# Filling batches of an attention loop: a new order inside each turn, rotating exponential banks, a wait on the third exponential, and weight preparation one turn earlier

## The chip, the cores and the metric

The kernel runs on one core of a Trainium2 chip. The metric is the device time of one execution in microseconds (us). The profile names the engines PE (matrix products), PEld (PE loading the stationary operand of a product), DVE (vector), ACT (activations), POOL (GpSimd) and SP (it issues most DMAs); "PEclk" or "granted clock" is the share of PE's full clock.

## The reference

One transformer block with adaptive layer norm, on 2048 rows of 512 numbers, all in 32-bit floats:

```python
mod = (_silu(c) @ w_mod).reshape(c.shape[0], 6, 1, -1)     # sa, ca, ga, sb, cb, gb
h = _layernorm(x) * (1 + ca) + sa
x = x + ga * attention(h)      # 32 query heads of 16, one key head, one value head, softmax, then @ wo
h = _layernorm(x) * (1 + cb) + sb
x = x + gb * (gelu(h @ w1 + b1) @ w2 + b2)                 # 512 -> 1376 -> 512
```

## The kernel before

**Units and turns.** The 2048 query rows are cut into 8 blocks of 256, and each block into 8 units of four heads: 64 units. A unit's scores are built transposed, 128 keys by 512 query columns at a time. The operands of a score product have 64 rows, so it uses one half of the PE array; `s` (0 or 1) says which half. Two products on different halves run at the same time, and two on the same half one after the other.

For each unit the loop from line 1289 takes the keys in steps: `K` counts 8 steps, two of them (`X`, `Y`) in one pass through the loop body. A pass has two **turns**. In each, PE gets products on both halves, side by side, and then `pv` (line 589), the 16 instructions `acc` that multiply the exponentials by the values; they use all rows of the array and write tile `acc`. The `pv` after the first turn is that of the step before, the one after the second turn is that of `X`.

The products of a turn are of three kinds:

- `sexp` (line 571): one product `e` (line 584), a bank of 512 scores, and at once `p` (line 587), its exponential on ACT. There are four in a turn. They use three banks, `e0`, `e1` and `e2`; the number is written out by hand where `sexp` is called (lines 1324 to 1348). A product into a bank waits for the ACT instruction that read the bank last.
- `Max.step` (line 483): one product `m` (line 490) for a *later* unit, whose softmax needs the maximum of each row first, and the reduction `mx` (line 495) on DVE. There are four in nearly every turn. Tag `m` has three banks, in rotation; each `m` waits for the reduction of the third `m` before it. When a unit's maxima are complete, `put_max` has POOL gather them and SP send them to rows of `qst`, from where the exponentials get them.
- `half` (line 179): **fillings**. All other matrix work (query projections `qps`, output projection `wops`, transposes `tp`, the two feed-forward layers `w1ps` and `w2ps`) is cut into batches of about six products of 512 columns. A batch's products have 128 rows; the first turn of a pass does rows 0 to 63 of each of them, on half 0, beside the score products of half 1, and the second turn does rows 64 to 127, on half 1, beside the score products of half 0. Both halves add to one PSUM bank. A turn without a batch is **plain** (`plain`, line 1308): it has only four `e` and about four `m`.

**What sets the order.** Every engine runs its instructions in the order in which they are written. `issue` (line 1260) merges two or more groups: it takes the next instruction of the group whose summed lengths are smallest, and the first group of those that tie. `mixture` (line 1270) alternates two lists. In a filled turn one group is the score half (`m`, `e`, `m`, `e`, `m`, `e`, `m`) and the other the six halves and then one `e`. `halves` (line 1302) gives the halves their lengths, with `AHEAD` = 0.75 for a full batch. The score group comes first, unless the batch begins a new bank. PE's order in a filled turn is then

```
m e h h m h e h m h h e e m        # h: a filling
```

where the thirteenth instruction, an `e`, runs on the fillings' half and the others, but for `h`, on the score half. After the last half batch of a bank, `resume` issues the instruction that empties the bank, mostly on DVE, and the reductions collected in `reduces` come behind it.

**Waits for weight pieces.** `clock` counts four ticks a pass. The first layer's weights are split into two parts in advance and kept in DRAM (`dw1`); `fetch_w1` (line 745) brings a piece back, and `heed` notes its DMA with a due tick (6 ticks later). `wait_early` (line 567) lets an `e` of the second turn of a pass wait for the first noted DMA that is due. `fetch_rest` (line 749) fetches the first three pieces, once for each block.

**Weight preparation.** `prep_w1`, `prep_wo` and `prep_w2` (lines 1029 to 1080) are advanced once a pass (every `PREP` = 4 ticks). In `prepare` (line 1018) piece `i` is loaded at one call, split on POOL (`work`) two calls later, and, for `w1`, sent to DRAM two calls after that. The staging tile has three buffers.

Of the kernel before, what the change touches and what calls it, by code (L numbers as in the profile page):

```python
# [47 lines left out]
def adaln_mqa_mlp(  # L48
# [127 lines left out]
        for ps, a, b_, first_, last_ in batch:  # L176
            nc.tensor.matmul(ps, a, b_, start=first_, stop=last_)  # L177

    def half(one, s):

        ps, a, b_, first_, last_ = one
        rows = slice(64 * s, 64 * s + 64)
        nc.tensor.matmul(ps, a[rows], b_[rows], start=first_ and s == 0, stop=last_ and s == 1)  # L183

    def ln_stats(xt, pool, n, between=None):
        st = pool.tile([P, n, 6], F32, name="st", tag="st", bufs=2)
# [369 lines left out]
    accs = {}  # L556
    heeded = []

    def wait_for(ins, other, reason):
        tc.add_manual_dep(ins.ins, other.ins.name, mybir.DependencyInfo(mybir.DependencyClass.Sync, mybir.DependencyReason.DATA),  # L560
                          reason=reason)

    def heed(dma, n):

        heeded.append((clock[0] + n, dma))

    def wait_early(ins):
        if heeded and heeded[0][0] <= clock[0]:
            wait_for(ins, heeded.pop(0)[1], "a weight piece")

    def sexp(u, K, j, s, bank):

        w = blocks[units[u][0]][1]
# [10 lines left out]
        ins = nc.tensor.matmul(e, ks[rows, kt * P:(kt + 1) * P], rhs, start=True, stop=True)  # L584
        if clock[0] % 4 == 2 and s == 0 and K % 2:
            wait_early(ins)
        nc.scalar.activation(ptiles[u, K][:, j, s, :], e, AF.Exp, scale=0.25)  # L587

    def pv(u, K):
        w = blocks[units[u][0]][1]  # L590
        if K == 0:
            accs[u] = psum.tile([P, w], F32, name=f"acc{u}", tag="v")
        pt = ptiles.pop((u, K))
        for kt in ([K] if w == 512 else [2 * K, 2 * K + 1]):
            for cidx in range(4):
                s, j = divmod(cidx, 2)
                rhs = pt[:, j, s, :] if w == 512 else pt[:, kt - 2 * K, s, j * w:(j + 1) * w]
                nc.tensor.matmul(accs[u][32 * cidx:32 * cidx + 32, :], va[:, kt, :], rhs,  # L598
                                 start=kt == 0, stop=kt == NKT - 1)

    def finish_unit(u):
        b, Q = units[u]
# [686 lines left out]
    for u in range(NU):  # L1289
        for K in range(0, steps[u], 2):  # L1290
            goal = lead[u] + (lead[u + 1] - lead[u]) * (K + 2) / steps[u]
            goal = min(goal, first[u + QBUFS] if u + QBUFS < NU else first[NU])
            n = max(0, 2 * round((goal - mp.done) / 2))

            def maxes(s, n, first_=1.0, held=None):
                return [(1.0 if i else first_, lambda i=i: mp.step(s, held if i == 2 else None)) if mp.has(s) else (0.0, lambda: None)
                        for i in range(n)]

            def exps(s, which):
                return [(1.0, lambda K=K, j=j, bank=bank: sexp(u, K, j, s, bank)) for K, j, bank in which]  # L1300
# [7 lines left out]
            def plain(s, K, t, n, banks):  # L1308

                a, b_, c_, d = banks  # L1310
                one = mixture(exps(s, [(K, 0, a), (K, 1, c_)]), maxes(s, n))
                other = maxes(t, n)
                if not holder and mp.has(t) and n > 1:
                    other[-1] = 1.0, lambda: mp.step(t, tag="x", bufs=1)
                issue(one, exps(t, [(K, 0, b_)]) + other + exps(t, [(K, 1, d)]))

            X, Y = K, K + 1

            due()
            batch = take() if behind else None
            if batch:
                groups = [mixture(maxes(1, n // 2, 0.0), exps(1, [(X, 0, 0), (X, 1, 1), (Y, 0, 2)])),
                          halves(batch, 0) + exps(0, [(X, 0, 0)])]
                issue(*(reversed(groups) if batch[0][3] else groups))
            else:
                plain(1, X, 0, (n + 2) // 4, (1, 2, 0, 1))
            clock[0] += 1
            due()  # L1330
            if behind:
                end_step(*behind)
            clock[0] += 1
            due()
            if batch:

                reduces = [] if batch[-1][4] else None

                def go_on_():
                    resume()  # L1340
                    for fn in reduces or ():
                        fn()

                issue(mixture(maxes(0, n // 2, 0.0, reduces), exps(0, [(X, 1, 0), (Y, 0, 1), (Y, 1, 2)])),
                      halves(batch, 1) + [(0.0, go_on_)] + exps(1, [(Y, 1, 0)]))
                advance()
            else:
                plain(1, Y, 0, n // 4, (2, 0, 1, 2))
            clock[0] += 1
            due()  # L1350
            end_step(u, X)
            behind = (u, Y)
            clock[0] += 1
            if state["mods"] and state["q"] == 0 and w2H is None:
                w2H = att.tile([P, NF, D], F32R, name="w2H", tag="bigH")
                w2L = att.tile([P, NF, D], F32R, name="w2L", tag="bigL")
                preps["w2"] = prep_w2()
            if clock[0] >= prepared[0] + PREP and weights and weights[0] in preps:
                prepared[0] = clock[0]
                if next(preps[weights[0]], 0) == 0:  # L1360
                    weights.pop(0)
# [51 lines left out]
```

## Time and profile before

| | us |
|---|---|
| three runs | 1591.32, 1591.73 (median), 1595.98 |
| the profiled execution | 1592.94 |
| its span in the trace | 1590.6 |
| the attention loop in it, from the first to the last of its turns | 82.7 to 1538.3 |

What the profiled execution took beyond its span, 2.3 us, lies around the trace. The trace's clock starts with the span. A row of a timeline has start, duration, engine, line, operation and the tile written and read, and in brackets how long the engine sat idle before it and what ended that. "PEld" rows are weight loads; a product's wait is on its load. The ends of PE's rows are modelled by the profiler.

### The profile page before, as it was taken

To read this page: it belongs to the slowest core of one execution; us is meant where nothing else is said; L and a number is where in the kernel's file an instruction comes from. 1 tells how busy PE (TensorE), PEld (TensorE's weight loads), DVE (VectorE), ACT (ScalarE), POOL (GpSimd) and SP (SyncE) were. 2 spreads that over 40 slices of the span, in tenths; PEclk is the share of its full clock that TensorE was granted. 3 is DMA by queue.
4 is the path that set the end of the run, shared out by engine and by line. 5 is a ranking of instruction groups with operands and counts; after the bars stand their busy time and mean duration, and the time that the engine had idled before them with its cause. 6 is when DMAs were issued, how large, how long until landed. Compare 5 with 4: busy or idle time off the path is not lost.

```text
span 1590.6 us, 41519 instructions
## 1 busy us (share of the span) xinstructions
PE 1563.0 (98%) x16369; PEld 1008.8 (63%) x16369; DVE 1410.8 (89%) x2473; ACT 1201.1 (76%) x2393; POOL 667.5 (42%) x1176
## 2 busy tenths in 40 slices
PE   6999999999999999999999999999999999999998
PEld 3466665557665676657666676656666576656667
DVE  7899999899999998999989999999999999999615
ACT  5577778778777887778877887778877787778853
POOL 4445434747422571246421462244612473225711
PEclk8999999999999999999999999999999999999999
DMA  7236312313020220303112120303112120212231
GB/s 250 82 113 214 105 68 70 128 39 101 17 98 31 68 69 25 103 18 107 32 49 79 54 85 22 106 14 98 43 37 89 45 96 19 95 39 63 81 134 73
DMA packets 83126, 121.62 MB, mean 76 GB/s; under 512 B 19614, under 2 KB 56222, under 8 KB 82676
## 3 DMA queue, kind: packets, MB, share of 16 engines
q1 hardware_dynamic: 82916, 118.97, 23.0%
q8 instruction: 129, 2.11, 0.6%
q14 instruction: 65, 0.53, 0.1%
q10 hardware_dynamic: 16, 0.00, 0.0%
HBM read 91.13 MB, written 27.27 MB: 74 GB/s over the span
## 4 chain that ended last, share of the span: by engine, by line
PE 88%; DVE 4%; POOL 4%; ACT 2%; DMA 1%; issue 1%; SPq 0%; POOLq 0%; DVEq 0%; ACTq 0%
PE acc L598 29%; PE m L490 21%; PE e L584 17%; PE w1ps L183 8%; PE w2ps L183 4%; DVE mx L495 3%; PE wops L183 2%; POOL xh L805 2%; PE qps L183 2%; PE w2ps L177 1%; PE w1ps L177 1%; ACT p L587 1%; PE tp L183 1%; PE kps L159 1%; POOL x L809 0%
## 5 line engine op out<-in xcount | busy, mean ns | idle before, releaser
L495 DVE TENSOR_REDUCE mx<-m 128x1 f32<-128x512 f32 x2048 | 1270.1, 681 | 101.4 <-PE m L490 73.8
L587 ACT ACTIVATE p<-e 128x512 f32<-128x512 f32 x2048 | 1067.2, 599 | 308.0 <-PE e L584 240.2
L490 PE MATMUL m<-ks,qst 64*128 64x512 f32 x2048 | 819.6, 424 | 6.1 <-ACT ks L393 2.3
L584 PE MATMUL e<-qst,ks 64*128 64x512 f32 x2048 | 739.1, 409 | 3.4 <-ACT p L587 1.5
L598 PE MATMUL acc<-p,va 128*32 128x256 f32 x8192 | 548.8, 385 | 0.0
L490 PEld LDWEIGHTS m<-ks,qst 64*128 64x128 f32 x2048 | 362.8, 184 | 168.8 <-DVE mx L495 145.2
L584 PEld LDWEIGHTS e<-qst,ks 64*128 64x128 f32 x2048 | 366.0, 184 | 91.2 <-ACT p L587 64.2
L598 PEld LDWEIGHTS acc<-p,va 128*32 128x32 f32 x8192 | 213.9, 109 | 218.9 <-issue 115.6
L183 PE MATMUL w1ps<-h2H,w1t 64*128 64x256 f32 x1232 | 236.7, 288 | 0.8
L539 POOL TENSOR_SCALAR mt<-turned 8x32 f32<-8x32 f32 x256 | 53.4, 209 | 400.6 <-DVE turned L545 388.6
L183 PEld LDWEIGHTS w1ps<-h2H,w1t 64*128 64x128 f32 x1232 | 184.1, 185 | 32.8 <-issue 23.3
L183 PE MATMUL w1ps<-h2L,w1t 64*128 64x256 f32 x616 | 169.6, 275 | 0.0
L183 PE MATMUL w2ps<-w2H,gH 64*128 64x512 f32 x286 | 118.0, 413 | 0.0
L183 PE MATMUL w2ps<-w2L,gH 64*128 64x512 f32 x286 | 117.3, 410 | 0.0
L183 PE MATMUL w2ps<-w2H,gL 64*128 64x512 f32 x286 | 117.3, 410 | 0.0
L183 PEld LDWEIGHTS w1ps<-h2L,w1t 64*128 64x128 f32 x616 | 113.5, 184 | 0.0
L906 POOL TENSOR_SCALAR tt<-tt 128x256 f32<-128x256 f32 x77 | 31.2, 405 | 162.5 <-ACT tt L905 159.3
L907 POOL TENSOR_TENSOR tt<-tt,z 128x256 f32<-128x256 f32 x77 | 57.1, 741 | 6.4
L134 POOL TENSOR_TENSOR gL<-z,gH 128x256 fp32r<-128x256 f32 x77 | 56.9, 739 | 6.4
L917 POOL TENSOR_TENSOR z<-tt,z 128x256 f32<-128x256 f32 x77 | 56.3, 731 | 6.0
L916 POOL TENSOR_TENSOR tt<-tt,z 128x256 f32<-128x256 f32 x77 | 56.8, 737 | 0.0
L183 PEld LDWEIGHTS w2ps<-w2H,gH 64*128 64x128 f32 x286 | 52.7, 184 | 5.9 <-DVE ot L953 2.5
(188 smaller groups left out, 1468.0 us busy)
## 6 DMA issues: line engine op xcount, KB each, us to landing
w1t<-dw SPq DMA_DIRECT2D x82, 512.0 KB
qst<-dq SPq DMA_DIRECT2D x384, 32.0 KB
do<-oc SPq DMA_DIRECT2D x64, 128.0 KB
dw<-w1s SPq DMA_DIRECT2D x11, 512.0 KB
xt<-in_A_x_dram SPq DMA_DIRECT2D x4, 1024.0 KB
dq<-qH SPq DMA_DIRECT2D x16, 256.0 KB
dq<-qL SPq DMA_DIRECT2D x16, 256.0 KB
x<-in_A_x_dram SPq DMA_DIRECT2D x8, 512.0 KB
```

The lines of the kernel that those rows point to most:

```text
L134: eng_l.tensor_tensor(out=dst_l, in0=src, in1=raw(dst_h), op=ALU.subtract)
L177: nc.tensor.matmul(ps, a, b_, start=first_, stop=last_)
L183: nc.tensor.matmul(ps, a[rows], b_[rows], start=first_ and s == 0, stop=last_ and s == 1)
L490: nc.tensor.matmul(m, qsts[u][rows, j, t * P:(t + 1) * P], ks[rows, kc * 512:(kc + 1) * 512], start=True, stop=True)
L495: nc.vector.tensor_reduce(out=self.mx[u][:, i, kc:kc + 1], in_=m, axis=AX.X, op=ALU.max)
L539: nc.gpsimd.tensor_scalar(out=mt[:, g:g + 32], in0=turned[g:g + 4 * T, :], scalar1=1.0, scalar2=0.0, op0=ALU.mult, op1=ALU.add)
L584: ins = nc.tensor.matmul(e, ks[rows, kt * P:(kt + 1) * P], rhs, start=True, stop=True)
L587: nc.scalar.activation(ptiles[u, K][:, j, s, :], e, AF.Exp, scale=0.25)
L598: nc.tensor.matmul(accs[u][32 * cidx:32 * cidx + 32, :], va[:, kt, :], rhs, start=kt == 0, stop=kt == NKT - 1)
L907: nc.gpsimd.tensor_tensor(out=tt, in0=tt, in1=z, op=ALU.mult)
L916: nc.gpsimd.tensor_tensor(out=tt, in0=tt, in1=z, op=ALU.mult)
L917: nc.gpsimd.tensor_tensor(out=z, in0=tt, in1=z, op=ALU.add)
```

## The change

Four edits, all in or for the loop:

1. **Order and banks.** `sexp` takes its bank from `ebank()`, which rotates through the three banks over all exponentials, in place of numbers written by hand. In a filled turn the fillings' group now always stands first. The score half is built by `scores`: `m e m e m`, then the remaining `m`, then the third `e`. The lengths in `halves` are now the same for all batches: together 4.5 of the score half's units, so that the `e` of the fillings' half comes ahead of the last `e` of the score half: it is the third of the turn's four exponentials. When a bank ends with the batch, the reductions of the third *and* fourth maximum are held until the bank's emptying is issued (before: of the third).
2. **The witness.** That third exponential is kept as `state["witness"]`. The first half product of each following half batch waits for it, except the very first of a bank.
3. **Weight pieces.** The waits move from `e` to products of `pv`, any due one is taken, and the due tick is 24 ticks after the fetch for a block's first three pieces and 8 for the others (before 6).
4. **Preparation.** The split of a piece comes one call after its load (before two), and its sending two calls after the split, as before.

In plain turns, the `m` that is put into bank `x` is the first of its half, no longer the last.

PE's order in a filled turn is now `h m e h m h e h h m h m e e`, with the thirteenth again on the fillings' half.

```diff
-AHEAD = 0.75
...
-    def half(one, s):
+    def half(one, s, behind=None):
 
         ps, a, b_, first_, last_ = one
         rows = slice(64 * s, 64 * s + 64)
-        nc.tensor.matmul(ps, a[rows], b_[rows], start=first_ and s == 0, stop=last_ and s == 1)
+        ins = nc.tensor.matmul(ps, a[rows], b_[rows], start=first_ and s == 0, stop=last_ and s == 1)
+        if behind is not None:
+            wait_for(ins, behind, "the other half of the array adds to the same bank")
...
     def wait_early(ins):
-        if heeded and heeded[0][0] <= clock[0]:
-            wait_for(ins, heeded.pop(0)[1], "a weight piece")
-
-    def sexp(u, K, j, s, bank):
+        for one in heeded:
+            if one[0] <= clock[0]:
+                heeded.remove(one)
+                wait_for(ins, one[1], "a weight piece")
+                break
+
+    def sexp(u, K, j, s):
...
-        e = psum.tile([P, 512], F32, name=f"e{u}_{K}_{j}_{s}", tag="x" if bank == "x" else f"e{bank}", bufs=1)
+        e = psum.tile([P, 512], F32, name=f"e{u}_{K}_{j}_{s}", **ebank())
...
-        ins = nc.tensor.matmul(e, ks[rows, kt * P:(kt + 1) * P], rhs, start=True, stop=True)
-        if clock[0] % 4 == 2 and s == 0 and K % 2:
-            wait_early(ins)
-        nc.scalar.activation(ptiles[u, K][:, j, s, :], e, AF.Exp, scale=0.25)
+        nc.tensor.matmul(e, ks[rows, kt * P:(kt + 1) * P], rhs, start=True, stop=True)
+        return nc.scalar.activation(ptiles[u, K][:, j, s, :], e, AF.Exp, scale=0.25)
...
-                nc.tensor.matmul(accs[u][32 * cidx:32 * cidx + 32, :], va[:, kt, :], rhs,
-                                 start=kt == 0, stop=kt == NKT - 1)
+                ins = nc.tensor.matmul(accs[u][32 * cidx:32 * cidx + 32, :], va[:, kt, :], rhs,
+                                       start=kt == 0, stop=kt == NKT - 1)
+                if kt % 2 and cidx:
+                    wait_early(ins)
...
-        heed(nc.sync.dma_start(out=raw(w1ts[f]), in_=dw1[f]), 6)
+        heed(nc.sync.dma_start(out=raw(w1ts[f]), in_=dw1[f]), 8 if f > 2 else 24)
...
-        for i in range(n + (4 if send else 2)):
-            if send and i >= 4:
-                send(i - 4)
-            if 2 <= i < n + 2:
-                work(i - 2)
+        for i in range(n + (3 if send else 1)):
+            if send and i >= 3:
+                send(i - 3)
+            if 1 <= i < n + 1:
+                work(i - 1)
...
-                return [(1.0 if i else first_, lambda i=i: mp.step(s, held if i == 2 else None)) if mp.has(s) else (0.0, lambda: None)
+                return [(1.0 if i else first_, lambda i=i: mp.step(s, held if i > 1 else None)) if mp.has(s) else (0.0, lambda: None)
...
-                total = products(batch)
-                ahead = AHEAD if total > BATCH - 0.5 else (BATCH - (1.5 if batch[-1][4] else 0.5)) / total
-                return [(ahead * products([one]), lambda one=one: half(one, s)) for one in batch]
+                ahead = (BATCH - 1.5) / products(batch)
+                behind_ = None if s == 0 and batch[0][3] else state["witness"]
+                return [(ahead * products([one]), lambda i=i, one=one: half(one, s, None if i else behind_))
+                        for i, one in enumerate(batch)]
+
+            def scores(s, which, held=None):
+
+                m, e = maxes(s, n // 2, 0.0, held), exps(s, which)
+                return mixture(m[:3], e[:2]) + m[3:] + e[2:]
...
-                    other[-1] = 1.0, lambda: mp.step(t, tag="x", bufs=1)
+
+                    other[0] = 1.0, lambda: mp.step(t, tag="x", bufs=1)
...
-                groups = [mixture(maxes(1, n // 2, 0.0), exps(1, [(X, 0, 0), (X, 1, 1), (Y, 0, 2)])),
-                          halves(batch, 0) + exps(0, [(X, 0, 0)])]
-                issue(*(reversed(groups) if batch[0][3] else groups))
+                issue(halves(batch, 0) + exps(0, [(X, 0)], True), scores(1, [(X, 0), (X, 1), (Y, 0)]))
...
-                issue(mixture(maxes(0, n // 2, 0.0, reduces), exps(0, [(X, 1, 0), (Y, 0, 1), (Y, 1, 2)])),
-                      halves(batch, 1) + [(0.0, go_on_)] + exps(1, [(Y, 1, 0)]))
+                issue(halves(batch, 1) + [(0.0, go_on_)] + exps(1, [(Y, 1)], True), scores(0, [(X, 1), (Y, 0), (Y, 1)], reduces))
```

More of the change, by code (lines that the diff above doesn't have):

```diff
@@ L1295, in maxes, with exps, one, plain @@
             def maxes(s, n, first_=1.0, held=None):
[L1296 removed]
+                return [(1.0 if i else first_, lambda i=i: mp.step(s, held if i > 1 else None)) if mp.has(s) else (0.0, lambda: None)
                         for i in range(n)]
[L1299 to L1312 removed]
+            def exps(s, which, witness=False):
+                def one(K, j):
+                    ins = sexp(u, K, j, s)
+                    if witness:
+                        state["witness"] = ins
+                return [(1.0, lambda K=K, j=j: one(K, j)) for K, j in which]
+            def halves(batch, s):
+                ahead = (BATCH - 1.5) / products(batch)
[5 more added lines that the diff above has]
+                return mixture(m[:3], e[:2]) + m[3:] + e[2:]
+            def plain(s, K, t, n):
+                one, other = maxes(s, n), maxes(t, n)
                 if not holder and mp.has(t) and n > 1:
[L1314 to L1315 removed]
+                    other[0] = 1.0, lambda: mp.step(t, tag="x", bufs=1)
+                issue(mixture(exps(s, [(K, 0), (K, 1)]), one), exps(t, [(K, 0)]) + other + exps(t, [(K, 1)]))
             X, Y = K, K + 1
@@ L1323, in adaln_mqa_mlp @@
             if batch:
[L1324 to L1326 removed]
+                issue(halves(batch, 0) + exps(0, [(X, 0)], True), scores(1, [(X, 0), (X, 1), (Y, 0)]))
             else:
[L1328 removed]
+                plain(1, X, 0, (n + 2) // 4)
             clock[0] += 1
@@ L1340, in go_on_ @@
                     resume()
-                    for fn in reduces or ():
-                        fn()
-                issue(mixture(maxes(0, n // 2, 0.0, reduces), exps(0, [(X, 1, 0), (Y, 0, 1), (Y, 1, 2)])),
-                      halves(batch, 1) + [(0.0, go_on_)] + exps(1, [(Y, 1, 0)]))
+                    while reduces:
+                        reduces.pop(0)()
+                issue(halves(batch, 1) + [(0.0, go_on_)] + exps(1, [(Y, 1)], True), scores(0, [(X, 1), (Y, 0), (Y, 1)], reduces))
+                assert not reduces
                 advance()
             else:
-                plain(1, Y, 0, n // 4, (2, 0, 1, 2))
+                plain(1, Y, 0, n // 4)
             clock[0] += 1
```

6 lines of the change are left out of this document (3 added, 3 removed).

## The prediction

> **What bounds the kernel now.** The page comes first, for the engines and the two costliest groups.
>
> ```profile
> span 1590.6 us, 41519 instructions
> PE 1563.0 (98%) x16369; PEld 1008.8 (63%) x16369; DVE 1410.8 (89%) x2473; ACT 1201.1 (76%) x2393; POOL 667.5 (42%) x1176
> ...
> L495 DVE TENSOR_REDUCE mx<-m 128x1 f32<-128x512 f32 x2048 | 1270.1, 681 | 101.4 <-PE m L490 73.8
> L587 ACT ACTIVATE p<-e 128x512 f32<-128x512 f32 x2048 | 1067.2, 599 | 308.0 <-PE e L584 240.2
> ```
>
> PE is busy throughout, so time is saved only where PE's own sequence gets shorter. One maximum takes DVE 0.68 us and one exponential takes ACT 0.60 us. The attention loop is a row of turns, each closed by 16 `acc` instructions, so the windows view over line 598 counts turns (x/16). The stretches below are filled, plain, filled, plain, plain, filled.
>
> ```profile
> 82.70:243.70 161.00, 59.86 (x896) 23.37 (x896) 1.00 0.37 122
> 243.70:291.30 47.60, 19.36 (x292) 7.51 (x288) 1.00 0.29 89
> 291.30:317.80 26.50, 9.31 (x128) 3.52 (x128) 0.94 0.40 131
> 317.80:328.60 10.80, 4.40 (x68) 1.67 (x64) 1.00 0.09 20
> ...
> 340.00:345.60 5.60, 2.19 (x36) 0.83 (x32) 1.00 0.08 21
> 345.60:500.60 155.00, 57.71 (x864) 22.54 (x864) 1.00 0.21 68
> ```
>
> A turn with a filling takes 155.0/54 = 2.87 us (161/56 = 2.87 in the first stretch). The eight turns from 291.3 took 26.5/8 = 3.31 us; more on them below. Plain turns number 18, and then 4 + 2 in each of seven passes: 60. The same view over line 490 counts the turns that also hold four maximum products:
>
> ```profile
> 82.70:1538.30 1455.60, 798.25 (x1984) 354.02 (x1984) 1.00 0.22 70
> ```
>
> 1984/4 = 496 turns, less 60 plain ones, leaves **436 filled turns**; nearly all of the change lies in them. The timeline of one:
>
> ```profile
> 802.82 0.50 PE L490 MATMUL m<-ks,qst 64*128 64x512 f32 x1
> 802.86 0.50 PE L183 MATMUL w2ps<-w2H,gH 64*128 64x512 f32 x1
> 803.15 0.39 PE L584 MATMUL e<-qst,ks 64*128 64x512 f32 x1
> 803.35 2.48 DVE L495 TENSOR_REDUCE mx<-m 128x1 f32<-128x512 f32 x4 [0.35 <-PE w2ps L183]
> 803.38 0.39 PE L490 MATMUL m<-ks,qst 64*128 64x512 f32 x1
> 803.38 0.18 PEld L584 LDWEIGHTS e<-qst,ks 64*128 64x128 f32 x1
> 803.58 2.13 ACT L587 ACTIVATE p<-e 128x512 f32<-128x512 f32 x4 [0.77 <-PE w2ps L183]
> ...
> 804.07 0.39 PE L584 MATMUL e<-qst,ks 64*128 64x512 f32 x1
> 804.23 0.18 PEld L584 LDWEIGHTS e<-qst,ks 64*128 64x128 f32 x1
> 804.23 0.18 PEld L490 LDWEIGHTS m<-ks,qst 64*128 64x128 f32 x1
> 804.30 0.43 PE L490 MATMUL m<-ks,qst 64*128 64x512 f32 x1
> 804.36 0.39 PE L584 MATMUL e<-qst,ks 64*128 64x512 f32 x1
> 804.67 1.07 PE L598 MATMUL acc<-p,va 128*32 128x256 f32 x16
> 805.67 0.18 PEld L490 LDWEIGHTS m<-ks,qst 64*128 64x128 f32 x1 [0.41 <-DVE mx L495]
> 805.76 0.18 PEld L183 LDWEIGHTS w2ps<-w2H,gH 64*128 64x128 f32 x1
> ```
>
> Two halves of the array work side by side. The score half runs m, e, m, e, m, e, m; the other runs six filling halves and one e. On a half, products start 0.23 us apart (803.15, 803.38), except that the first is followed after 0.33: **a load that nothing covers costs about 0.10**. The seven starts of the score half therefore lie at 0, 0.33, 0.56, 0.79, 1.02, 1.25 and 1.48 us. A turn is then 1.85 us of products and 1.00 of `acc`.
>
> Two waits show. ACT ends at 803.58 + 2.13 = 805.71, and only then can the next turn's first e load, since it has the bank of the exponential just finished; the filling is queued behind it and loads at 805.76, 0.09 after m. And the last e loads at 804.23, 0.05 after the first exponential of its turn (803.58 + 0.60 = 804.18), whose bank it reuses.
>
> **The change, part by part.**
>
> *Rotating banks, fillings first.* The first e of a turn takes the bank of the second exponential of the turn before, long read, so the 0.09 goes. The last e now takes the bank of this turn's first exponential, so its load still cannot come before 1.41 us and the turn cannot end before 2.84: the fastest turns now, such as that between the last two loads in the next fence, 811.49 to 814.33. The gain is bounded by 2.87 - 2.84 = 0.03 a turn, 13 us in all.
>
> *The witness.* The first filling of each half batch, unless it begins a bank, waits for the third exponential of the turn before. Behind it on PE stands the whole turn. Its product is the seventh of its half: start 1.48, end 1.87, on ACT by 1.91 (the 0.04 between the e that ends at 803.54 and ACT at 803.58), done at 2.51, seen at 2.56. The next turn starts at 2.84 or later. Cost taken: nothing; the cover is 0.28 us, and a later ACT beyond it would be paid one for one, with no gain possible.
>
> *The new order of the score half.* The groups are now issued as m, e, m, e, m, **m, e**: the fourth maximum moves from the seventh place to the sixth. There are three m banks, so the fourth waits for the first maximum of its own turn. That one starts on DVE at 0.53 (803.35 - 802.82) and takes 0.68: 1.21. How soon a load follows, and what a late one costs, a turn with a disturbed DVE shows:
>
> ```profile
> 808.07 3.67 DVE L495 TENSOR_REDUCE mx<-m 128x1 f32<-128x512 f32 x6
> 808.59 0.49 PE L490 MATMUL m<-ks,qst 64*128 64x512 f32 x1
> ...
> 810.00 0.18 PEld L490 LDWEIGHTS m<-ks,qst 64*128 64x128 f32 x1 [0.19 <-DVE mx L495]
> 810.07 0.18 PEld L584 LDWEIGHTS e<-qst,ks 64*128 64x128 f32 x1
> 810.49 1.07 PE L598 MATMUL acc<-p,va 128*32 128x256 f32 x16
> 811.49 0.18 PEld L490 LDWEIGHTS m<-ks,qst 64*128 64x128 f32 x1 [0.41 <-DVE mx L495]
> ...
> 814.33 0.18 PEld L490 LDWEIGHTS m<-ks,qst 64*128 64x128 f32 x1 [0.41 <-DVE mx L495]
> ```
>
> The six maxima are (3.67 - 0.68)/5 = 0.60 apart; the third, this turn's first, ends at 808.07 + 1.20 + 0.68 = 809.95, and the load comes at 810.00: 0.05 later. Now the fourth m in its new place: loaded at 1.21 + 0.05 = 1.26, where covered loads stand at 1.02; running 0.10 later, at 1.36, not at 1.25. The third e is behind it on the same half: 1.36 + 0.23 = 1.59. From a last product to `acc` I take 0.34 (load 804.23, so running at 804.33, `acc` at 804.67). The turn is 1.59 + 0.34 + 1.00 = **2.93 us, 0.06 more than now**; in the old seventh place the load at 1.26 was just in time. Bounds: nothing, if the late load is absorbed (2.84), to a load wholly exposed at its 0.18 (3.01). I take 0.10, which the first load of every turn shows. Over 436 turns: +26.2 us.
>
> Where DVE also empties a 512-wide bank, the first maximum of the next turn is later. Three groups of these lie in the loop (of the x16, two each are in the tail):
>
> ```profile
> L953 DVE TENSOR_TENSOR ot<-w2ps,x 128x512 f32<-128x512 f32 x16 | 11.1, 691 | 23.6 <-PE w2ps L183 15.9 <-PE w2ps L177 7.8
> L786 DVE TENSOR_TENSOR x<-wops,x 128x512 f32<-128x512 f32 x16 | 11.1, 691 | 2.3 <-PE wops L183 1.2 <-PE wops L177 0.8 <-PE m L490 0.2
> ...
> L441 DVE COPY q<-qps 128x512 f32<-128x512 f32 x14 | 9.7, 691 | 0.2
> ```
>
> That makes 42 turns. In the example the maximum ended at 809.95 - 808.59 = 1.36, less 0.06 for the longer turn ahead: 1.30, so 0.09 beyond the 1.21 already counted: +3.8 us. (Such turns were dearer before too; that is within the mean of 2.87.)
>
> The Trainium skill, "TensorE: Matmul & The Clock Gate", Part 3, "What overlaps and what doesn't", says that a weight load overlaps running matmuls only if its row group differs. By that rule the late load is exposed in full, 0.18 us, with the sum of the second rival below. The trace is against it: at 803.38 an e loads while m of the same half runs.
>
> *Weight pieces awaited later.* The waits of line 585 on the first fetched pieces stall PE in the eight turns from 291.3:
>
> ```profile
> 301.90 0.18 PEld L584 LDWEIGHTS e<-qst,ks 64*128 64x128 f32 x1 [1.43 <-DMA w1t<-dw]
> ...
> 303.18 0.22 PEld L584 LDWEIGHTS e<-qst,ks 64*128 64x128 f32 x2 [0.75 <-DMA w1t<-dw]
> ```
>
> With 24 ticks (twelve turns, 34 us) instead of 6 the pieces have landed: 8 x (3.31 - 2.87) = -3.5 us, the slower clock there (0.94) included. Later fetches show no such wait, so 8 instead of 6 is nothing.
>
> *Preparation a turn sooner.* Loads, splits and sends keep their number. A split now follows its load by two turns (5.7 us), not four. The longest wait of this kind now:
>
> ```profile
> POOL w2f L1077 <- DMA w2f<-in_B_w_dram: 3.7, 1, 3.7
> ```
>
> Behind a waiting split stand the gathers of the maxima on POOL, and behind those, SP's sends of them; the exponentials that need them start most of a unit (eight turns) later. That cover takes a delay of 3.7 us. Taken: nothing; if it failed, about 3.7 us at a unit boundary. Plain turns keep their order but for which maximum has bank x: nothing.
>
> **Sum.** +26.2 + 3.8 - 3.5 = +26.5 us on the profiled execution's 1592.9 us: 1619.4. That execution stands 1.2 us above the median of the runs, 1591.7, so I predict **1618 us**.
>
> **Rivals.**
>
> *The late load is absorbed.* If the first maximum is seen early enough, by about 1.15 instead of 1.26, or PE has slack that I miss, all filled turns fall to 2.84: 436 x -0.03 = -13.1, -3.5 more: 1575 us. For it: the waits that go are real. Against it: 0.53 + 0.68 is the same in every turn, however the turn before ran.
>
> *The late load is exposed in full.* Turns of 3.01: 436 x 0.14 = +61.0, with +3.8 - 3.5: 1653 us. Against it: the 0.33 after the first product.
>
> *The witness binds.* It decides from the point where the third exponential is seen after the turn's end, 0.37 us later than reckoned for a turn of 2.93. Activations of the feed-forward stand at the head of ACT's turns and could do that; ACT now waits 0.77 us there, which speaks against it. At 0.1 us in every turn it would be +44 us beyond the forecast: 1661.
>
> *Gain and loss cancel*, or the new order does not bite: 0.03 gained, about as much lost: 1588 to 1595.
>
> **How the numbers follow.** Forecast 0.68; absorbed 0.14; exposed in full 0.07; witness 0.05; cancelled 0.06. About 0.3% (5 us) is what a measurement here can tell from no change. Faster by more: 0.14; within: 0.05; slower: 0.81 (the forecast, the two dear rivals and 0.01 of the cancelled). The range, 1594 to 1645, takes the forecast, the near edge of the cancelled case and the partial forms of the dear ones; the absorbed case and the full dear ones stay out.
>
> **What would show it.** In the changed profile: filled turns of 2.93 us (54 in 158 us); the load of the fourth m 0.05 after the end of the turn's first maximum, with DVE named, and the third e last of the turn at 1.59; no filling loading late behind ACT; no wait on `w1t` at 300 us. If the fourth m loads later than the maximum allows, or turns take 2.84, the prediction is wrong.

## The result, and the profile after

| | median of the runs, us | lowest to highest | against the kernel before, 95% interval |
|---|---|---|---|
| before | 1591.73 (5 runs) | 1590.94 to 1596.12 | |
| after | 1631.85 (5 runs) | 1629.71 to 1632.43 | 1.0238 [1.0219, 1.0258] |
| predicted | 1618 | range 1594 to 1645 | |

The changed kernel is slower, by 40 us; the prediction had +26. The profiled execution took 1629.71 us, 36.8 more than that of before. First the page of the kernel after, with the lines that answer to those of before:

```profile
span 1627.6 us, 41427 instructions
PE 1604.5 (99%) x16369; PEld 972.6 (60%) x16369; DVE 1413.4 (87%) x2473; ACT 1236.5 (76%) x2393; POOL 665.2 (41%) x1176
...
L500 DVE TENSOR_REDUCE mx<-m 128x1 f32<-128x512 f32 x2048 | 1269.9, 683 | 134.5 <-PE m L495 86.4
L589 ACT ACTIVATE p<-e 128x512 f32<-128x512 f32 x2048 | 1102.3, 597 | 312.2 <-PE e L588 231.8
```

The engines' work is the same: as many products (16369), maxima (2048 of 683 ns, before of 681) and exponentials (2048 of 597 ns, before of 599). (In the kernel after, `m` is line 495, its maximum 500, `e` 588, its exponential 589, the half fillings 186, `acc` 600.) So the time is not in a longer maximum or exponential. DVE sat idle ahead of its maxima for 134.5 us instead of 101.4: it waits more, so it isn't the engine that fills the time either. What got longer is the turn. The windows view of the kernel after over the `acc` products (now line 600), for turns with `qps`, `wops`, `w1ps` and `w2ps` fillings, and between them one plain turn (the columns are start:end, length, busy PE and busy PEld with their counts, PEclk, DMA share, GB/s):

```profile
83.17:250.16 166.99, 59.96 (x900) 23.37 (x896) 1.00 0.36 118
297.16:321.41 24.25, 8.57 (x132) 3.34 (x128) 1.00 0.40 132
329.34:331.94 2.60, 1.07 (x20) 0.42 (x16) 1.00 0.20 51
349.19:413.99 64.80, 23.55 (x356) 9.18 (x352) 1.00 0.25 81
413.99:485.57 71.58, 25.69 (x388) 10.02 (x384) 1.00 0.20 65
```

The PEld count divided by 16 gives the turns. With `qps` they take 166.99/56 = 2.982 us, with `w1ps` 64.80/22 = 2.945, with `w2ps` 71.58/24 = 2.983. The same stretches of the kernel before:

```profile
82.74:243.72 160.98, 59.88 (x896) 23.37 (x896) 1.00 0.37 122
325.77:328.62 2.85, 1.15 (x20) 0.42 (x16) 1.00 0.00 0
345.63:408.81 63.18, 23.49 (x352) 9.18 (x352) 1.00 0.26 83
408.81:477.53 68.72, 25.70 (x388) 10.02 (x384) 1.00 0.20 66
```

2.875, 2.872 and 2.863. So the three kinds lost 0.107, 0.073 and 0.120 a turn, where 0.06 was predicted for all. Both traces cut at the starts of all turns give the whole account:

| us, by what the turn is filled with | before | after | difference |
|---|---|---|---|
| `qps`, 56 turns | 161.0 | 167.0 | +6.0 |
| `wops`, 56 | 165.1 | 167.4 | +2.3 |
| `tp`, 28 | 79.7 | 83.4 | +3.7 |
| `w1ps`, 154 (2 of them in the tail, without `m`) | 441.0 | 453.3 | +12.3 |
| `w2ps`, 156 (12 of them in the tail, without `m`) | 446.3 | 462.5 | +16.2 |
| plain, 60 | 162.5 | 158.2 | -4.3 |
| the first turn, which holds the kernel's beginning | 73.8 | 74.2 | +0.4 |

That is +36.6 of the span's +37.0. Of the 436 filled turns with four maxima, 284 have wide fillings and 152 narrow ones (`w1ps`). Now one turn of each sort from the timeline of the kernel after. First one with wide fillings (512 columns: `qps`, `wops`, `tp`, `w2ps`):

```profile
464.75 0.18 PEld L186 LDWEIGHTS w2ps<-w2L,gH 64*128 64x128 f32 x1 [0.41 <-ACT p L589]
464.75 0.50 PE L186 MATMUL w2ps<-w2L,gH 64*128 64x512 f32 x1
464.75 0.18 PEld L495 LDWEIGHTS m<-ks,qst 64*128 64x128 f32 x1
464.75 0.49 PE L495 MATMUL m<-ks,qst 64*128 64x512 f32 x1
...
465.32 2.48 DVE L500 TENSOR_REDUCE mx<-m 128x1 f32<-128x512 f32 x4 [0.49 <-PE w2ps L186]
...
466.06 0.18 PEld L495 LDWEIGHTS m<-ks,qst 64*128 64x128 f32 x1 [0.33 <-DVE mx L500]
...
466.72 1.07 PE L600 MATMUL acc<-p,va 128*32 128x256 f32 x16
...
467.72 0.18 PEld L186 LDWEIGHTS w2ps<-w2H,gL 64*128 64x128 f32 x1 [0.41 <-ACT p L589]
```

The prediction's marker is there: the load at 466.06 is the fourth `m`, late, with the first maximum of its own turn (465.32 + 0.68 = 466.00) as its releaser, 0.06 after it. From it to `acc` are 0.66, within 0.01 of the reckoned 0.10 + 0.23 + 0.34, and `acc` takes its 1.00. But DVE starts 0.57 after the turn does, not 0.53. The turn is 2.97 long. Then one with narrow fillings (256 columns, `w1ps`), again after:

```profile
363.92 0.18 PEld L495 LDWEIGHTS m<-ks,qst 64*128 64x128 f32 x1
...
364.45 1.29 DVE L500 TENSOR_REDUCE mx<-m 128x1 f32<-128x512 f32 x2
...
365.20 0.18 PEld L495 LDWEIGHTS m<-ks,qst 64*128 64x128 f32 x1
...
365.86 1.07 PE L600 MATMUL acc<-p,va 128*32 128x256 f32 x16
```

DVE starts at 0.53 here, the late load stands at 1.28, `acc` at 1.94: a turn of 2.94, a hundredth from the 2.93 predicted.

The two theories at this point. **The first maximum:** every filled turn waits, by way of the fourth `m`, for the end of its own first maximum; and in the 284 wide turns that maximum also starts 0.04 later, because its `m` is issued behind a filling that ends at the same moment (0.50 and 0.49 above). **The rivals:** the witness and ACT, whose name stands at the fillings' loads; or the rotation of the banks; or a sum of small losses in the side edits.

### The profile page after: what moved, and what is told of

It is laid out like the page before. It is cut to its first block, busy times and chain, and to the rows that moved or that the text cites. A ratio compares the mean times of both kernels' runs of the same rounds, so it can differ in the third digit from the quotient of the medians.

```text
span 1627.6 us, 41427 instructions
## 1 busy us (share of the span) xinstructions
PE 1604.5 (99%) x16369; PEld 972.6 (60%) x16369; DVE 1413.4 (87%) x2473; ACT 1236.5 (76%) x2393; POOL 665.2 (41%) x1176
## 4 chain that ended last, share of the span: by engine, by line
PE 94%; DVE 3%; ACT 1%; DMA 1%; POOL 0%; issue 0%; SPq 0%; ACTq 0%; POOLq 0%; DVEq 0%
PE acc L600 30%; PE e L588 17%; PE m L495 15%; PE w2ps L186 9%; PE w1ps L186 9%; PE wops L186 4%; PE qps L186 4%; DVE mx L500 2%; PE w2ps L176 1%; PE tp L186 1%; PE w1ps L176 1%; PE kps L158 1%; PE modr L284 0%; DMA qst<-ml 0%; DMA wm<-in_w_mod_dram 0%; DVE st L797 0%
## 5 line engine op out<-in xcount | busy, mean ns | idle before, releaser
L500 DVE TENSOR_REDUCE mx<-m 128x1 f32<-128x512 f32 x2048 | 1269.9, 683 | 134.5 <-PE m L495 86.4
L589 ACT ACTIVATE p<-e 128x512 f32<-128x512 f32 x2048 | 1102.3, 597 | 312.2 <-PE e L588 231.8
L495 PE MATMUL m<-ks,qst 64*128 64x512 f32 x2048 | 803.9, 441 | 6.3 <-ACT ks L398 2.4
L588 PE MATMUL e<-qst,ks 64*128 64x512 f32 x2048 | 695.9, 406 | 0.8 <-DMA qst<-ml 0.8
L588 PEld LDWEIGHTS e<-qst,ks 64*128 64x128 f32 x2048 | 321.9, 184 | 49.5 <-ACT p L589 38.8
L186 PEld LDWEIGHTS w2ps<-w2L,gH 64*128 64x128 f32 x286 | 52.7, 184 | 26.3 <-ACT p L589 21.5
L186 PEld LDWEIGHTS w2ps<-w2H,gH 64*128 64x128 f32 x286 | 52.7, 184 | 26.2 <-ACT p L589 13.2
L186 PEld LDWEIGHTS w2ps<-w2H,gL 64*128 64x128 f32 x286 | 52.7, 184 | 25.9 <-ACT p L589 15.7
L911 POOL TENSOR_TENSOR tt<-tt,z 128x256 f32<-128x256 f32 x77 | 56.5, 734 | 6.4
```

What stands on the lines that cost most here:

```text
L186: ins = nc.tensor.matmul(ps, a[rows], b_[rows], start=first_ and s == 0, stop=last_ and s == 1)
L495: nc.tensor.matmul(m, qsts[u][rows, j, t * P:(t + 1) * P], ks[rows, kc * 512:(kc + 1) * 512], start=True, stop=True)
L500: nc.vector.tensor_reduce(out=self.mx[u][:, i, kc:kc + 1], in_=m, axis=AX.X, op=ALU.max)
L589: return nc.scalar.activation(ptiles[u, K][:, j, s, :], e, AF.Exp, scale=0.25)
L911: nc.gpsimd.tensor_tensor(out=tt, in0=tt, in1=z, op=ALU.mult)
```

## The experiments

Times are medians of the runs, beside the kernel before on the same chip. "Old order" is the score half `m e m e m e m`.

**First maximum cut, and, as a control, the fourth.** In every filled turn one maximum reduces only 256 of its 512 columns; the rest is left out, and in both kernels the exponentials' scale is 0.0025 instead of 0.25, so that they stay finite. What they compute isn't the block any more; the time is what they are for.

```diff
-                nc.vector.tensor_reduce(out=self.mx[u][:, i, kc:kc + 1], in_=m, axis=AX.X, op=ALU.max)
+                nc.vector.tensor_reduce(out=self.mx[u][:, i, kc:kc + 1], in_=m[:, :cols], axis=AX.X, op=ALU.max)
...
-                return [(1.0 if i else first_, lambda i=i: mp.step(s, held if i > 1 else None)) if mp.has(s) else (0.0, lambda: None)
+                return [(1.0 if i else first_, lambda i=i: mp.step(s, held if i > 1 else None, 256 if i == short else 512)) if mp.has(s) else (0.0, lambda: None)
...
-                m, e = maxes(s, n // 2, 0.0, held), exps(s, which)
+                m, e = maxes(s, n // 2, 0.0, held, 0), exps(s, which)    # 3 in place of 0 for the fourth
```

> The changed kernel, but in each filled turn the first of the four maxima reduces 256 of its 512 columns (the exponentials are scaled down so that they stay finite: the result is not the reference's). Theory 1, the fourth m waits in its new place for the first maximum: that ends about 0.27 us earlier, at 1.00 instead of 1.26, the fourth m loads unhindered at 1.03, and only the last e's wait for the first exponential is left: filled turns of 2.84 to 2.86 us, 436 x 0.11 = 48 us less, about 1583 us. Theory 2, the filling's wait for the third exponential sets the turn: no change, 1630 us.

> The same cut at the fourth maximum instead of the first (same work taken from DVE, the result again not the reference's). Theory 1: the fourth m still waits for the whole first maximum, turns stay at 2.94 to 2.98; a few us less at most, where DVE is late from the turn before: 1625 to 1632 us. Rival, DVE's load as such makes the turns long: as much gained as with the first maximum cut, about 1583 us. Theory 2: 1630 us.

With the first maximum cut: 1584.29 us (one run; before 1593.17). With the fourth: 1627.46 (one run). The same DVE time is saved in both; only that of the first maximum counts, and it takes out 47.6 us against the changed kernel's median (in the traces the 436 filled turns lose 47.8). The windows of the kernel with the first cut, `qps`, `w1ps`, `w2ps`:

```profile
84.36:244.50 160.14, 59.96 (x900) 23.38 (x896) 1.00 0.37 121
341.77:404.39 62.62, 23.56 (x356) 9.18 (x352) 1.00 0.27 83
404.39:473.49 69.10, 25.69 (x388) 10.02 (x384) 1.00 0.21 66
```

2.860, 2.846 and 2.879 a turn: with the fourth `m` in its new place but the first maximum early, turns come near the bound of 2.84 that the prediction had worked out. Witness, rotation and preparation are all in this kernel, so none of them by itself makes the 40 us.

**Score half issued first.** The changed kernel with the two groups of `issue` swapped, in both turns of a pass:

```diff
-                issue(halves(batch, 0) + exps(0, [(X, 0)], True), scores(1, [(X, 0), (X, 1), (Y, 0)]))
+                issue(scores(1, [(X, 0), (X, 1), (Y, 0)]), halves(batch, 0) + exps(0, [(X, 0)], True))
...
```

> The changed kernel with the score half's group issued first in every filled turn, so that m stands ahead of the first filling. In the changed kernel's 512-wide turns the first maximum starts on DVE at 0.57, not at 0.53 as before and as in its 256-wide turns. If that comes from the filling ahead of m (both end together, and their signals come one after the other), the 284 wide turns fall by 0.04: 11 us less, about 1621 us, with the first maximum at 0.53 again. If the order of the groups is immaterial: 1632 us, start at 0.57.

1620.59 us (4 runs, 1619.26 to 1622.69), 1.0174 [1.0159, 1.0189] of before. A turn with wide fillings from its timeline:

```profile
472.81 0.18 PEld L495 LDWEIGHTS m<-ks,qst 64*128 64x128 f32 x1 [0.41 <-issue]
472.81 0.49 PE L495 MATMUL m<-ks,qst 64*128 64x512 f32 x1
...
473.35 2.48 DVE L500 TENSOR_REDUCE mx<-m 128x1 f32<-128x512 f32 x4 [0.44 <-PE m L495]
...
474.09 0.18 PEld L495 LDWEIGHTS m<-ks,qst 64*128 64x128 f32 x1 [0.28 <-DVE mx L500]
...
475.74 0.18 PEld L495 LDWEIGHTS m<-ks,qst 64*128 64x128 f32 x1 [0.41 <-issue]
```

The product `m` is as long as in the kernel after (0.49), yet DVE starts at 0.54, the late load stands at 1.28 and the turn is 2.93: the predicted turn. The name at DVE is `m` here and was the filling `w2ps` in the turn above, but the name decides nothing: in the next turn of the kernel after (467.72) the profile names `m`, and DVE starts 0.57 after the start there too. The start is what moved: issue order alone gives the 0.04 back in wide turns. Together they take 837.9 us instead of 846.3, 8.4 less where 11 were expected; part of what is missing is in the turns behind an emptied bank, which take as long as in the kernel after (2.99).

**The new order alone.** The kernel before, with `scores` in place of `mixture` in the two filled turns, the fourth reduction held as well, and the halves' lengths of the kernel after; no witness, banks numbered by hand, no side edits.

```diff
-                groups = [mixture(maxes(1, n // 2, 0.0), exps(1, [(X, 0, 0), (X, 1, 1), (Y, 0, 2)])),
+                groups = [scores(maxes(1, n // 2, 0.0), exps(1, [(X, 0, 0), (X, 1, 1), (Y, 0, 2)])),
...
```

> The kernel before, with the new order of the score half (and the one length rule for the halves) alone; banks by hand, scores first, no witness, old weight waits and preparation. Theory 1: the fourth m loads at 1.27 and the turn takes 2.93: 436 x 0.055 = +24 us and some 4 us in the turns after DVE has emptied a bank, about 1620 us. Theory 2, the witness costs the time: this kernel has none, so 1592 us or, since the first e's bank is free earlier, down to 1580 us.

1628.28 us (4 runs), 1.0219 [1.0202, 1.0237]. Its turns:

```profile
86.09:251.81 165.72, 59.97 (x900) 23.37 (x896) 1.00 0.36 117
353.08:417.84 64.76, 23.49 (x352) 9.18 (x352) 1.00 0.26 80
417.84:488.33 70.49, 25.68 (x388) 10.01 (x384) 1.00 0.21 66
```

2.959, 2.944, 2.937: those of the experiment before it (2.961, 2.943, 2.941 by the same view), which has the score half first too. So the order makes the loss by itself. The time is 8 us above that expected: the kernel before is 1.4 us dearer on this chip, and the 436 filled turns went from a mean of 2.876 to 2.952, which is 33 us and not the 28 expected. What separates it from the experiment before it, 7.7 us, is mostly the side edits that it lacks: its plain turns take 163.5 us and not 158.4, and its `wops` turns 167.5 and not 165.8.

**The old order put back, twice.** The changed kernel with the score half as before; once the witness is its last exponential, the third of the turn, and once it stays with the fillings' exponential, which in this order is the fourth. In both only the reduction of the third maximum is held, as before the change.

```diff
-                return mixture(m[:3], e[:2]) + m[3:] + e[2:]
+                return mixture(m, e)
...                                       # from here on: the first of the two kernels alone
-                    if witness:
+                    if witness and (K, j) == which[-1]:
...
-                ahead = (BATCH - 1.5) / products(batch)
+                ahead = (BATCH - 1.8) / products(batch)
...
-                m, e = maxes(s, n // 2, 0.0, held), exps(s, which)
+                m, e = maxes(s, n // 2, 0.0, held), exps(s, which, mp.has(s))
...
```

> The changed kernel with the fourth m back in the seventh place of the score half (m e m e m e m). The third exponential of a turn is then the score half's last one; it comes behind the last filling in PE's order, for which the halves take 4.2 instead of 4.5 units, and it is the one that the next turn's fillings wait for. All else as changed. Theory 1: late m gone, rotation's gain kept: filled turns of 2.84 to 2.85 us, 436 x 0.12 = 52 us less, 1575 to 1582 us, faster than the kernel before by about 1%. Rival, the fillings issued first or the wait on the third exponential keep a cost of their own: over 1592 us.

> The same old order, but the halves keep 4.5 units and the next fillings wait for the exponential of the fillings' half, which is then the fourth of the turn. Its matmul starts at 1.52, so ACT ends at about 2.87, and a filling that stands first in the next turn is free at 2.92 instead of 2.84. If a wait on the fourth exponential binds: turns of 2.91 to 2.93, about 1610 us. If the wait costs nothing wherever it is put: as with the third, 1575 to 1582 us.

The shorter lengths in the first put its witness, the score half's last exponential, behind the last filling in PE's order; by the code that changes nothing for batches of six products, but it does for narrow ones. With the third exponential: 1588.18 us (6 runs), 0.9967 [0.9955, 0.9978]. With the fourth: 1614.46 (4 runs), 1.0130 [1.0115, 1.0145]. Putting the fourth `m` back, as in the first, undoes the whole loss, with a witness, rotation and side edits in place. That kernel still missed its expectation (it is 6 to 13 us dearer): its wide turns keep 0.02 to 0.04 above the 2.85 of its narrow ones; with `w2ps` they take

```profile
407.00:475.95 68.95, 25.69 (x388) 10.02 (x384) 1.00 0.21 65
```

68.95/24 = 2.873. And with the fourth exponential the witness does bind. Its timeline:

```profile
463.97 2.06 ACT L589 ACTIVATE p<-e 128x512 f32<-128x512 f32 x4 [0.88 <-PE e L588]
...
465.06 1.07 PE L600 MATMUL acc<-p,va 128*32 128x256 f32 x16
466.09 0.18 PEld L186 LDWEIGHTS w2ps<-w2H,gL 64*128 64x128 f32 x1 [0.45 <-ACT p L589]
```

The fourth exponential ends at 463.97 + 2.06 = 466.03, the next turn loads at 466.09, 1.03 after `acc` began and not 1.00. The wide turns of this kernel sum to 836.4 us, those of the one with the third exponential to 817.2. This tells how to read the name "ACT p" at the fillings' loads of the kernel after. The waits views of that kernel, and of the one with the fourth exponential (engine, what waits, what for: us in total, times, the longest):

```profile
PEld w2ps L186 <- ACT p L589: 50.4, 122, 0.5
```

```profile
PEld w2ps L186 <- ACT p L589: 54.5, 122, 0.5
```

50.4/122 = 0.41 is what every turn shows between the last load of `acc` and the first of the next turn, whichever name stands there (with the score half first it is "issue"). 54.5/122 = 0.45 is a wait. In the kernel after no filled turn has more than 0.43 there, so its witness doesn't bind. Taking the witness's wait alone out of the changed kernel was not tried.

**Old order, score half first.** The kernel with the third exponential, with the swap of groups shown above.

> The kernel with the fourth m back in the seventh place and the fillings waiting for the third exponential, and the score half's group first in each filled turn. In the run with the fillings first, narrow turns took 2.85 us as expected, but the wide ones 2.87: the first exponential sometimes came at 1.43 instead of 1.37, the first maximum at 0.57 instead of 0.53. If the filling in front of m and e delays their signals: wide turns of 2.845 us, 284 x 0.025 = 7 us less, about 1581 us. If it is something else: unchanged at 1588 us.

1580.09 us (4 runs, 1578.84 to 1580.45), 0.9906 [0.9891, 0.9921]: faster than both kernels. A turn with wide fillings, and the windows of `qps`, `w1ps`, `w2ps`:

```profile
464.25 0.18 PEld L495 LDWEIGHTS m<-ks,qst 64*128 64x128 f32 x1 [0.41 <-DVE mx L500]
...
464.78 2.48 DVE L500 TENSOR_REDUCE mx<-m 128x1 f32<-128x512 f32 x4 [0.36 <-PE m L495]
...
465.01 2.06 ACT L589 ACTIVATE p<-e 128x512 f32<-128x512 f32 x4 [0.25 <-PE w2ps L186]
...
465.66 0.18 PEld L588 LDWEIGHTS e<-qst,ks 64*128 64x128 f32 x1 [0.20 <-ACT p L589]
...
466.09 1.07 PE L600 MATMUL acc<-p,va 128*32 128x256 f32 x16
```

```profile
84.78:244.59 159.81, 59.95 (x900) 23.37 (x896) 1.00 0.37 122
341.95:404.55 62.60, 23.55 (x356) 9.18 (x352) 1.00 0.25 83
404.55:472.78 68.23, 25.70 (x388) 10.02 (x384) 1.00 0.21 67
```

The maximum has left the path: the last load of the turn is an `e` at 1.41, released 0.05 after the first exponential (465.01 + 0.60 = 465.61), and the next turn begins at 466.09 + 1.00 = 467.09: 2.84, the bound of the rotation. The means are 2.854, 2.846 and 2.843. This kernel is 14.2 us below before on its chip; the side edits alone make 7.2 of that (below), so 7 are left to what else differs: the rotating banks, the witness, the halves' lengths, and the score half first also where a batch begins a bank. These were not tried one by one. The changed kernel lies 40.1 us above before, the kernel with the third exponential 5.7 below it, and this one 14.2 below: the new place of the fourth `m`, with the small edits that go with putting it back, cost some 46 us, and fillings first another 8 or 9.

**The side edits.** Alone on the kernel before: the weight pieces' waits (edit 3); in plain turns the first `m` into bank `x`, not the last; the preparation (edit 4); and all three together.

```diff
-        heed(nc.sync.dma_start(out=raw(w1ts[f]), in_=dw1[f]), 6)
+        heed(nc.sync.dma_start(out=raw(w1ts[f]), in_=dw1[f]), 8 if f > 2 else 24)
```

> The kernel before with the waits for weight pieces moved to the value products and due after 24 or 8 ticks; nothing else. Expected: no wait on w1t at 300 us, the eight turns there at 2.87 instead of 3.32, 3.5 us less: about 1589 us. Rival: the pieces land so late that another instruction waits: 1592 us.

```diff
-                    other[-1] = 1.0, lambda: mp.step(t, tag="x", bufs=1)
+                    other[0] = 1.0, lambda: mp.step(t, tag="x", bufs=1)
```

> The kernel before, and in plain turns the maximum that goes into bank x is the first of its half, not the last; nothing else. The changed kernel's 60 plain turns took 4.3 us less than before, its last ones before a filled turn 2.61 instead of 2.84. If the filling behind a plain turn waited for the late reduction of bank x: these turns fall by 0.2 us, 14 of them, 2 to 4 us less, about 1589 us. If the rotating banks of the exponentials did it: no change, 1592 us.

```diff
-        for i in range(n + (4 if send else 2)):
+        for i in range(n + (3 if send else 1)):
```

> The kernel before with the weight preparation one call sooner behind its load, nothing else. As costed in the prediction: no change, 1592 us, with POOL waiting some us more for loads between 90 and 320 us. Rival: POOL's waits delay the gathered maxima and PE with them: some turns of over 3.3 us between 100 and 330 us, 1595 us or more.

> The kernel before with the three edits that leave the filled turns alone: weight pieces awaited later, preparation a turn sooner, bank x for the first maximum in plain turns. If they add up as seen singly: 3.5 us from the eight turns at 300 us and 3.6 us from the plain turns: about 1586 us. If the sooner preparation makes POOL wait for its loads and that reaches PE: over 1590 us.

| on the kernel before | us | before, same chip |
|---|---|---|
| weight pieces | 1590.76 (1 run) | 1593.84 (1590.95 to 1595.53) |
| bank `x` in plain turns | 1586.70 (1 run) | 1593.84 |
| preparation | 1591.91 (1 run) | 1594.33 (1593.16 to 1597.71) |
| all three | 1587.14 (5 runs), 0.9956 [0.9944, 0.9969] | 1594.33 |

The bank `x` edit has the effect that the prediction missed. Before, the last plain turn ahead of a filled one took 2.85 (the row 325.77:328.62 above), and after, 2.60 (329.34:331.94): by the code, the filling that begins bank `x` has to wait for the reduction of the `m` that had the bank last. That `m` was the last of its half and the third of the turn's four. In the kernel before:

```profile
325.40 4.45 DVE L495 TENSOR_REDUCE mx<-m 128x1 f32<-128x512 f32 x7
...
328.58 0.18 PEld L183 LDWEIGHTS tp<-ident,xh 64*128 64x128 f32 x1 [0.61 <-POOL x L809]
```

The fifth of the seven maxima, the turn's third, ends at 325.40 + 2.40 + 0.68 = 328.48, and the filling loads 0.10 later; the name POOL is no sign of the cause, since all 15 such turns load this long after their third maximum, whatever name stands there. With this edit alone these 15 turns take 2.60 to 2.62 us instead of 2.79 to 3.07, and the plain turns sum to 158.9 us instead of 162.5.

The weight pieces: the stretch of eight `wops` turns, 26.5 us before, with the later waits alone:

```profile
291.21:315.69 24.48, 8.49 (x128) 3.34 (x128) 1.00 0.44 142
```

That is 2.1 us less. No wait on `w1t` is left, but one of 1.3 us on another DMA (`qst<-ml`) is. With the preparation alone, the first turn, which holds the kernel's beginning, and the eight turns:

```profile
8.90:85.82 76.92, 1.07 (x16) 0.42 (x16) 0.89 0.44 153
294.31:317.34 23.03, 8.50 (x128) 3.34 (x128) 1.00 0.44 139
```

The eight turns take 3.5 us less, as with all three edits (23.04), and there is no wait on `w1t`, though the waits are where they were. So the sooner preparation alone removes the whole stall; the two other kernels with the old preparation and the old waits (the new order alone, and bank `x` alone) still have it, with 25.5 and 24.8 us. The time of 1591.91 hides this, because the first turn took 76.9 us at a granted clock of 0.89, where before it took 73.8 at 0.93; the new order alone, which lacks the edit, shows 77.0 there. How the sooner preparation lets the pieces land in time was not followed up.

## Why the prediction was right on the sign and short on the size

- **The new order**: right as a mechanism. The fourth `m` waits for its own turn's first maximum and loads 0.05 to 0.07 after it; a late load costs 0.10 (0.66 from it to `acc`, as reckoned, in the wide turn above). The size of one number in it was off. "That one starts on DVE at 0.53" was read in a turn whose score half was issued first; the change itself puts the fillings first, and then DVE starts at 0.57 in wide turns. The load stands at 1.31, not 1.26, the turn is 2.98, not 2.93. 284 wide turns x 0.05 = +14 us; the 152 narrow ones, 2.945 instead of 2.93, another +2. The prediction had the new order of PE in hand, `h m e ...`, and took the start of DVE from the old one.
- **After an emptied bank**: predicted 0.09 more in 42 turns, +3.8. Measured in the kernel after: 2.99 (median of the wide turns behind such an emptying) against 2.975 for other wide ones, 0.015, or +0.6. The next fence has one: the turn begins at 449.65, DVE comes from the emptying without a pause, and the first maximum is the third of the six, ending at 449.04 + 1.20 + 0.68 = 450.92: 1.27 after the start, only 0.02 later than in the wide turn above. The two delays cover each other. With the score half issued first, where the median of the other wide turns is 2.94, such turns take mostly 2.98 to 3.03 (median 2.99): there 0.05 of the predicted 0.09 shows.

```profile
448.44 0.68 DVE L957 TENSOR_TENSOR ot<-w2ps,x 128x512 f32<-128x512 f32 x1
...
449.04 3.67 DVE L500 TENSOR_REDUCE mx<-m 128x1 f32<-128x512 f32 x6
449.65 0.18 PEld L495 LDWEIGHTS m<-ks,qst 64*128 64x128 f32 x1
```

- **Weight pieces and preparation**: predicted -3.5 for the later waits and 0 for the sooner preparation. No wait on `w1t` is left in the kernel after between 295 and 325 us, and the eight turns take 24.25 us; at the 2.98 of its other wide turns they would take 23.8, so about 0.4 of the gain is missing. The term came out, but by luck as to its cause: alone, the later waits gave 2.1 of it and the preparation all 3.5. "Taken: nothing" was wrong for the preparation.
- **Plain turns**: predicted 0, measured -4.3. "Plain turns keep their order but for which maximum has bank x: nothing" failed; which maximum has the bank sets when the next filling can begin it.
- **The witness**: predicted 0, and right: the idle time ahead of the fillings is 0.41 in all filled turns, and with a witness in place turns fall to 2.84. In the wide turn shown above the third exponential ends at 467.23, 0.49 before the next turn starts. A wait on the fourth, which ends about when the next turn starts, costs 26 us in the old order.
- **The rotation** was taken as worth up to 0.03 a turn, and the new order hid it. In the old order with the score half first, turns of 2.84 come out; how much of the 7 us there is the rotation's was not separated.
- **POOL's longer waits** for the sooner splits: predicted to cost 0, and nothing in these turns shows a cost. A split waits 4.0 us for its load at the longest in the kernel after, where 3.7 was reckoned with:

```profile
POOL w2f L1081 <- DMA w2f<-in_B_w_dram: 6.6, 2, 4.0
```

The sum by these steps: 26.2 + 16 + 0.6 - 3.1 - 4.3 = +35.4, of 36.8 measured in the profiled executions; the rest, 1.4, isn't assigned. Of the rivals, the load exposed in full (1653) would have put 0.18 + 0.23 + 0.34 = 0.75 between the late load and `acc`; the row has 0.66, and loads beside running products of the same half are in every turn, as in the prediction's rows at 803.38. That rival was the rule of the Trainium skill, "TensorE: Matmul & The Clock Gate", Part 3, "What overlaps and what doesn't"; this case's trace is against it. The absorbed load (1575) failed because the load came at 1.28 to 1.31, where it needed 1.15.

## What to carry to other kernels

Before you move a product forward in a rotation of few buffers, work out when its buffer comes free in the same turn, and take that time from the order *after* the change: of two products that end together, the consumer of the one issued second started 0.03 to 0.04 us late here. Then put the product that a waiting engine needs ahead of the one that nobody waits for; here that swap alone took 8 us out of the 284 wide turns, in both pairs of kernels (846.3 to 837.9, and 817.2 to 809.2). And read a releaser's name together with the length of the idle time: a name with the idle time that every turn has is no wait. Last, try side edits one by one and read their own stretch of the trace: here the gain forecast for one came from another, and the total didn't show it.

## What the runs showed of the hardware

Two products of 0.49 and 0.50 us, on the two halves of the array and started together, let DVE begin 0.53 to 0.54 us after the start if the product it needs is issued first, and 0.56 to 0.57 if it is issued second; narrow fillings, which end earlier (a product of 0.38), leave it at 0.53 to 0.54 although they are issued first. The Trainium skill, "TensorE: Matmul & The Clock Gate", Part 3, "The cost: per-tile semaphore tail", says that the completion signals of products on different tiles are written one after another, at about 26 ns each; the 0.03 to 0.04 us seen here are near that, though no run here shows the signals themselves. That the swap of the issue order removes the delay is shown; that the signals queue is argued.
